# The filter network of a long-convolution kernel, fed by feature instead of by position

## The chip, the cores and the metric

The kernel runs on one core of a Trainium2 chip. The metric is the device time of one execution, in microseconds (us). The times shown are medians of several executions, and the profile is of one execution taken by the hardware profiler. The engines are named as the profile names them: PE is TensorE's matmul side and PEld its weight loads, DVE is VectorE, ACT is ScalarE, POOL is GpSimd, SP is SyncE, which here only issues transfers. A name with a "q" behind it (SPq, ACTq) is the issuing of a transfer from that engine's queue.

## What is computed

A long convolution and, on its result, a feed-forward block. Cut to what matters, with 2 sequences of 12480 positions and 128 channels:

```python
h_filt = (np.maximum(pos_emb @ w1, 0.0) @ w2) * np.exp(-0.01 * pos)[:, None]   # the filter, 12480 x 128
u = x * v
y = causal_convolution(u, h_filt)          # along positions, a channel at a time, by FFT
x2 = (x * y).reshape(24960, 128)
h = x2 @ w_in                              # 128 -> 2048
g = (a0 + a1*h + a2*h**2 + a3*h**3) / (1 + |b0|*|h| + |b1|*h**2 + 1e-6)
out = g @ w_out                            # 2048 -> 128
```

pos_emb is 12480 x 64, w1 is 64 x 64, w2 is 64 x 128. The two weights w_in and w_out come as 64-bit floats and are turned into 32-bit ones on the chip. The exponential decay falls below the smallest 32-bit float, so only the first 82 runs of 128 positions have a filter other than zero.

## The kernel before, in words

The work is in three stretches.

**The filter stretch** is the loop at L534 to L557 of the program. Position 128*m + n2 is held as row m (82 rows, `MF`) and residue n2 (128 of them, in two sides: 64 to 127, and 63 down to 0). A block `i` is four residues of each side (`NP` = 4), so there are 16 blocks. A block goes through these steps:

- `load_pos` (L274 to L282) loads the 82 rows of the positional embedding for four residues of each side, position on the partitions. It is four transfers from SP (a load of 80 rows and one of 2, for each side).
- `hf_w` (L480 to L489) multiplies by the decay on DVE, in two instructions, one a side. The decay (`win`) was loaded once, at L285.
- `hf_t` (L491 to L506) turns the block with four PE transposes, so that the 2 x 64 features lie on the partitions and 4 x 82 = 328 positions along the row. ACT copies it out of PSUM (L506).
- `hf_1` (L508 to L512) multiplies by w1 (twice on the diagonal of `bdw1`), and ACT takes the relu out of PSUM (L512). The decay is positive, so it can stand before the relu.
- `hf_2` (L514 to L524) multiplies by w2 with sum and difference of the two sides (`bdw2`), and four ACT instructions put the result into `hf`.

In iteration i the program issues `hf_t(i)`, `hf_1(i-1)` and `hf_2(i-2)`; it has 18 iterations. Every engine executes its own instructions in the order in which they are written, so what else is written in this loop stands in the same queues:

- `scalars` (L369 to L445), a generator, works out the constants of the rational function from moe_a and moe_b by a chain of tiny DVE instructions on 128x1 columns of the tile `sc`, with ACT for absolute values and a square root. Two of its steps stand in each iteration.
- `weights_gen` (L447 to L472), another generator, converts the weights in 16 pieces of 128x256. Step k: `to_f32` (L326 to L345) of piece k is seven DVE instructions (four one-input integer ones in 0.28 us each at L333, L335, L336, L339, another at L341, and two-input ones at L338 and L342) and a POOL addition (L344); `normal` (L349) of piece k-1 on DVE; for the first eight pieces two ACT instructions (L462, L463) that scale and round piece k-1 to `win_h`; and a POOL subtraction (L458) that leaves the remainder of piece k-2 in `win_l`. One step stands in each iteration from i = 5 on, so 13 of the 18 steps (k = 0 to 12) lie in this stretch. The tile `fa` has two buffers: L342 of piece k writes where L458 of piece k-2 read.
- `load_u` and `mult_u` load pieces of x and v and multiply them, on POOL (L248) for i < 8.
- PSUM is one pool of four tiles of two banks, used in turn.

**The convolution of sequence 0** (L602 to L643) runs over 32 groups of four channels, with a pipeline of four stages. Its DVE instructions are L173, L174, L205, L206, L566, L567 and L571 to L574, and in its first 24 iterations also a piece of x times v (L248, on DVE there). Steps of `weights_gen` that are left are taken in the iterations after that (L640).

**The second part** (L649 on) does the convolution of sequence 1 and the feed-forward block of both sequences by a fixed plan of work items.

A weight-step's end and the filter's end meet in the DVE queue: the convolution's first DVE instruction (L566) is queued behind the last weight step of the filter stretch, and needs the whole of `hf` through PE (L155).

Of the kernel before, what the change touches and what calls it, by code (L numbers as in the profile page):

```python
# [9 lines left out]
F32 = mybir.dt.float32  # L10
# [11 lines left out]
M = 98  # L22
# [40 lines left out]

def constants():
# [31 lines left out]
    win = win.reshape(M, N2)[:96]  # L96
# [14 lines left out]
def build(ctx: ExitStack, tc, x, x_q, v_q, pos_emb, w1, w2, w_in, w_out, moe_a, moe_b,  # L111
# [148 lines left out]
    with ExitStack() as st:  # L260
# [4 lines left out]
        win, bdw1, bdw2 = flat[0][0:96, 0:N2], flat[1][:, 0:128], flat[2][:, 0:2 * D]  # L265
# [5 lines left out]
        NPL = 4  # L271
        pos_t = {}

        def load_pos(p0):  # L274
            t = sp.tile([M, 2 * NPL, FO], F32, tag="wa", name="pos", bufs=3)
            for o, t0 in ((0, H2 + p0), (NPL, H2 - p0 - NPL)):
                if MF < M:
                    for r0, r1 in ((0, MF // 16 * 16), (MF // 16 * 16, MF)):
                        nc.sync.dma_start(out=t[r0:r1, o:o + NPL], in_=rows(pos_emb, r0, r1 - r0, t0, NPL, 0, FO))
                else:  # L280
                    load_rows(t[:, o:o + NPL], pos_emb, t0, NPL, 0, FO, True)
            pos_t[p0] = t  # L282
# [43 lines left out]
        def to_f32(raw, n):  # L326
# [4 lines left out]
            fa = sp.tile([128, n], F32, tag="f", name="f", bufs=2)  # L331
# [29 lines left out]

        def ts(o, i, s1, op0, s2=None, op1=None):
            kw = {} if op1 is None else {"op1": op1}
            nc.vector.tensor_scalar(out=col(o), in0=col(i), scalar1=s1, scalar2=s2, op0=op0, **kw)

        def tt(o, i, j, op):
            nc.vector.tensor_tensor(out=col(o), in0=col(i), in1=col(j), op=op)

        def scalars():  # L369


            for i in range(4):
                col(f"a{i}")
            for i in range(2):
                col(f"b{i}")
            nc.scalar.dma_start(out=sc[:, 0:4], in_=moe_a.unsqueeze(0).to_broadcast([128, 4]))
            nc.scalar.dma_start(out=sc[:, 4:6], in_=moe_b.unsqueeze(0).to_broadcast([128, 2]))
            for n in ("a0", "a1", "a2", "a3", "b0", "b1"):
                nc.scalar.activation(out=col("m" + n), in_=col(n), func=AF.Abs)
            tt("sum", "ma0", "ma1", ALU.add)  # L380
            tt("sum", "sum", "ma2", ALU.add)
            tt("sum", "sum", "ma3", ALU.add)
            yield

            ts("d", "ma3", 1e-30, ALU.max)
            nc.vector.reciprocal(out=col("d"), in_=col("d"))
            tt("q", "ma2", "d", ALU.mult)
            tt("q", "q", "ma2", ALU.mult)
            ts("lim", "sum", 16.0, ALU.mult)
            tt("flag", "q", "lim", ALU.is_le)  # L390
            ts("q", "ma3", 1024.0, ALU.mult)
            tt("q", "q", "sum", ALU.is_ge)
            yield
            tt("flag", "flag", "q", ALU.mult)
            ts("q", "mb1", 1e-9, ALU.is_ge)
            tt("flag", "flag", "q", ALU.mult)
            ts("q", "mb1", 1e9, ALU.is_le)
            tt("flag", "flag", "q", ALU.mult)
            tt("q", "mb0", "mb0", ALU.mult)
            ts("lim", "mb1", 16.0, ALU.mult)  # L400
            tt("q", "q", "lim", ALU.is_le)
            tt("flag", "flag", "q", ALU.mult)
            yield
            ts("not", "flag", -1.0, ALU.mult, 1.0, ALU.add)

            tt("b1e", "mb1", "flag", ALU.mult)
            tt("b1e", "b1e", "not", ALU.add)
            tt("a3e", "a3", "flag", ALU.mult)
            tt("a3e", "a3e", "not", ALU.add)
            yield  # L410

            for o, i in (("eta", "b1e"), ("sb1", "mb1")):
                ts("d", i, 1e-30, ALU.max)
                nc.scalar.activation(out=col("d"), in_=col("d"), func=AF.Ln)
                nc.scalar.activation(out=col(o), in_=col("d"), func=AF.Exp, scale=0.5)
                for _ in range(2):
                    nc.vector.reciprocal(out=col("d"), in_=col(o))
                    tt("d", "d", i, ALU.mult)
                    tt("d", "d", o, ALU.add)
                    ts(o, "d", 0.5, ALU.mult)  # L420
                yield
# [25 lines left out]
        def weights_gen():  # L447
# [663 lines left out]
```

## Time and profile before

| what | value |
|---|---|
| three runs | 2212.48, 2213.13 (median), 2214.62 us |
| the profiled execution: time | 2212.58 us |
| its span from first to last instruction | 2210.8 us |
| busy: PE, DVE, ACT, POOL | 89%, 93%, 87%, 91% of the span |
| filter stretch (up to the first L566) | 78.5 us |

The last 1.8 us of the time lie outside of the span. The shares are means over three stretches that differ. A row of the timeline reads: start in us, duration in us, engine, line, operation, tile written <- tiles read, shape, and in brackets how long the engine had been idle before it and what ended that. A row of the windows reads: the stretch, its length, then for PE, PEld, DVE, ACT and POOL the busy us and the number of instructions, the granted TensorE clock (1.00 is 2.4 GHz, 0.50 is 1.2 GHz), the mean busy share of the 16 DMA engines, and GB/s.

### The profile page before, as it was taken

The numbers are of one execution on the slowest core, as the hardware profiler recorded it, in microseconds if no ns is written. First come the engines' busy times: TensorE is split into PE (matmuls) and PEld (weight loads), VectorE is DVE, ScalarE is ACT, GpSimd is POOL, SyncE is SP. The second block draws the span as 40 slices with busy tenths as digits, with TensorE's granted clock in tenths as the row PEclk, the third lists the DMA queues.
The fourth block names the chain that finished last, engine by engine and source line by source line (L and its number), as shares of the span: only waits on it lengthen the run. The fifth ranks groups of instructions, "written<-read, shape, count | busy, mean of one in ns | idle before, by whom it ended". The sixth has DMA issues, their size and how long they took to land.

```text
span 2210.8 us, 25117 instructions
## 1 busy us (share of the span) xinstructions
PE 1966.8 (89%) x8352; PEld 1316.6 (60%) x8352; DVE 2067.0 (93%) x2354; ACT 1918.0 (87%) x1939; POOL 2015.8 (91%) x1605
## 2 busy tenths in 40 slices
PE   6899987899999999999999888888888888888886
PEld 4678766566666666666666555545545544555543
DVE  6899994899999998999999899999999999999997
ACT  5422223999999999999999899999999999999997
POOL 5477755999999999999999789999999999999998
PEclk9999988999999999999999999999999999999999
DMA  5344325443143233222222121221112111221100
GB/s 162 109 134 156 114 82 143 113 99 77 37 114 86 52 81 87 75 67 75 56 62 53 49 48 32 48 48 33 41 37 39 48 31 33 48 49 33 36 10 10
DMA packets 148283, 149.61 MB, mean 68 GB/s; under 512 B 88766, under 2 KB 117824, under 8 KB 145264
## 3 DMA queue, kind: packets, MB, share of 16 engines
q1 hardware_dynamic: 141120, 124.16, 22.4%
q10 hardware_dynamic: 7024, 23.76, 3.3%
q8 instruction: 68, 1.11, 0.2%
q14 instruction: 71, 0.58, 0.1%
HBM read 99.72 MB, written 48.17 MB: 67 GB/s over the span
## 4 chain that ended last, share of the span: by engine, by line
POOL 39%; ACT 20%; DVE 16%; PE 9%; issue 4%; DMA 0%; POOLq 0%; DVEq 0%; ACTq 0%
POOL v L986 20%; POOL v L980 9%; ACT v L915 5%; ACT r L964 4%; ACT l L959 4%; POOL q L954 4%; DVE q L970 4%; PE acc L995 3%; DVE q L975 3%; DVE v L925 3%; ACT q L891 3%; ACT q L943 3%; POOL q L953 2%; PE cv L823 2%; PE h L881 1%
## 5 line engine op out<-in xcount | busy, mean ns | idle before, releaser
L986 POOL TENSOR_TENSOR v<-v,q 128x970 f32<-128x970 f32 (+3 forms) x416 | 935.1, 2253 | 13.6 <-DVE q L975 12.7
L995 PE MATMUL acc<-v,wout 128*128 128x485 f32 (+3 forms) x1664 | 766.7, 584 | 126.3 <-POOL v L986 118.4
L925 DVE SCALAR_TENSOR_TENSOR v<-v,sc,h 128x970 f32<-128x970 f32 (+3 forms) x416 | 502.5, 1208 | 24.3 <-ACT q L891 22.5
L970 DVE SCALAR_TENSOR_TENSOR q<-q,sc,r 128x970 f32<-128x970 f32 (+3 forms) x416 | 502.1, 1207 | 22.7 <-ACT r L964 20.1
L995 PEld LDWEIGHTS acc<-v,wout 128*128 128x128 f32 x1664 | 293.6, 192 | 372.8 <-POOL v L986 183.6
L975 DVE SCALAR_TENSOR_TENSOR q<-q,r 128x970 f32<-128x970 f32 (+3 forms) x416 | 479.2, 1152 | 11.1
L881 PE MATMUL h<-ahi,win_l 128*128 128x486 f32 (+3 forms) x832 | 410.5, 493 | 45.8 <-DVE v L925 42.9
L915 ACT ACTIVATE v<-h,sc 128x970 f32<-128x970 f32 (+3 forms) x416 | 437.6, 1085 | 14.0 <-PE h L883 13.8
L964 ACT ACTIVATE r<-l 128x970 f32<-128x970 f32 (+3 forms) x416 | 416.6, 1001 | 16.9 <-DVE q L975 15.9
L980 POOL TENSOR_SCALAR v<-v,sc 128x980 f32<-128x980 f32 (+6 forms) x321 | 421.1, 1312 | 0.1
L959 ACT ACTIVATE l<-q,sc 128x1940 f32<-128x1940 f32 (+3 forms) x208 | 400.7, 1927 | 2.4 <-POOL q L954 2.1
L882 PE MATMUL h<-alo,win_h 128*128 128x486 f32 (+3 forms) x832 | 320.2, 385 | 0.0
L883 PE MATMUL h<-ahi,win_h 128*128 128x486 f32 (+3 forms) x832 | 318.9, 383 | 0.0
L891 ACT ACTIVATE q<-h 128x970 f32<-128x970 f32 (+3 forms) x303 | 303.3, 1001 | 2.8 <-POOL v L986 2.3
L881 PEld LDWEIGHTS h<-ahi,win_l 128*128 128x128 f32 x832 | 158.0, 190 | 208.6 <-DVE v L925 135.2
L882 PEld LDWEIGHTS h<-alo,win_h 128*128 128x128 f32 x832 | 158.8, 191 | 49.5 <-issue 34.2
L943 ACT ACTIVATE q<-q,sc 128x1940 f32<-128x1940 f32 (+2 forms) x95 | 185.6, 1953 | 0.0
L883 PEld LDWEIGHTS h<-ahi,win_h 128*128 128x128 f32 x832 | 158.8, 191 | 26.0
L948 ACT ACTIVATE q<-q,sc 128x1470 f32<-128x1470 f32 (+3 forms) x113 | 170.3, 1507 | 0.0
L823 PEld LDWEIGHTS cv<-yc,gt 90*98 90x98 f32 x1004 | 119.9, 165 | 26.2 <-issue 10.9
L823 PE MATMUL cv<-yc,gt 90*98 90x128 f32 x1004 | 128.1, 274 | 3.8 <-DVE an L829 3.5
L954 POOL TENSOR_TENSOR q<-q 128x490 f32<-128x490 f32 (+3 forms) x113 | 111.0, 982 | 9.4
(113 smaller groups left out, 2623.6 us busy)
## 6 DMA issues: line engine op xcount, KB each, us to landing
yc<-y_d SPq DMA_DIRECT2D x23, 900.0 KB
gt<-in_g_dram SPq DMA_DIRECT2D x48, 344.5 KB
xq<-in_x_q_dram SPq DMA_DIRECT2D x64, 196.0 KB
vq<-in_v_q_dram SPq DMA_DIRECT2D x64, 196.0 KB
h_d<-hg ACTq DMA_DIRECT2D x32, 360.0 KB
y_d<-ys ACTq DMA_DIRECT2D x16, 720.0 KB
hg<-h_d SPq DMA_DIRECT2D x64, 180.0 KB
y_d<-ys SPq DMA_DIRECT2D x16, 720.0 KB
```

Source lines behind the costliest of these rows:

```text
L881: nc.tensor.matmul(out=t[:, k, 0:w], lhsT=wl, rhs=hi[:, 0:w], start=True, stop=False)
L882: nc.tensor.matmul(out=t[:, k, 0:w], lhsT=wh, rhs=lo[:, 0:w], start=False, stop=False)
L883: nc.tensor.matmul(out=t[:, k, 0:w], lhsT=wh, rhs=hi[:, 0:w], start=False, stop=True)
L915: nc.scalar.activation(out=v, in_=st_h[s, i], func=AF.Square, bias=col("s"))
L925: stt(out=v, in0=v, scalar=col("k"), in1=h, op0=ALU.add, op1=ALU.mult)
L959: nc.scalar.activation(out=part(st_l, s, i), in_=part(st_q, s, i), func=AF.Ln, **({"bias": col("ka")} if short else {}))
L964: nc.scalar.activation(out=t[:, :, 0:w], in_=halves(st_l[s], i, w), func=AF.Exp, scale=-1.0)
L970: nc.vector.scalar_tensor_tensor(out=q, in0=q, scalar=col("ka") if short else 0.0, in1=st_r[s, i], op0=ALU.add, op1=ALU.mult)
L975: nc.vector.scalar_tensor_tensor(out=q, in0=q, scalar=2.0, in1=st_r.pop((s, i)), op0=ALU.subtract, op1=ALU.mult)
L980: nc.gpsimd.tensor_scalar(out=v, in0=v, scalar1=col("p0" if short else "a0"), scalar2=1.0, op0=ALU.add, op1=ALU.mult)
L986: nc.gpsimd.tensor_tensor(out=v, in0=v, in1=halves(st_q[s], i, w), op=ALU.mult)
L995: nc.tensor.matmul(out=acc[j][:, 0:w], lhsT=wout[:, f, :], rhs=st_v[s][:, i, 0:w], start=(f == 0), stop=(f == NF - 1), skip_group_check=True)
```

## The change

The positional embedding and the decay are laid out by feature on the host: `pos_q` has for each of the 16 blocks a 128 x 328 array (side and feature on the partitions, positions along the row), and `win_d` has for each block and side one row of 328 decay values. A block is now loaded with three transfers: the 128 x 328 piece of `pos_q`, and for each side the decay row, repeated over 64 partitions. There are no transposes, no copy of them and no `hf_w`: PE multiplies the loaded piece by `bdw1`, and one DVE instruction takes relu and decay out of PSUM together. The loop has 17 iterations, with `hf_1(i)` and `hf_2(i-1)` in iteration i.

Beside that: the loads of moe_a and moe_b go first on the ACT queue; `scalars` is rewritten with two-operation instructions (39 on DVE in three steps, one step an iteration); `to_f32` has one DVE instruction less; `fa` has three buffers; the remainder `win_l` moves from POOL to DVE as one instruction that scales and subtracts; L462 goes; the weight steps start at i = 3, so that 14 of the 18 (k = 0 to 13) lie in this stretch; `ident` is loaded late.

```diff
         def load_pos(i):
+            if i < nb:
+                t = sp.tile([128, W], F32, tag="wa", name="pos", bufs=3)
+                w = sp.tile([128, W], F32, tag="wn", name="win", bufs=3)
+                nc.sync.dma_start(out=t, in_=pos_q[i])
+                for s in range(2):
+                    nc.sync.dma_start(out=w[s * FO:(s + 1) * FO], in_=win_d[i, s].unsqueeze(0).to_broadcast([FO, W]))
+                pos_t[i] = (t, w)
...
+        nc.scalar.dma_start(out=sc[:, 0:4], in_=moe_a.unsqueeze(0).to_broadcast([128, 4]))
+        nc.scalar.dma_start(out=sc[:, 4:6], in_=moe_b.unsqueeze(0).to_broadcast([128, 2]))
         load_pos(0)
-        nc.sync.dma_start(out=win, in_=win_d)
-        nc.sync.dma_start(out=ident, in_=ident_d)
-        load_pos(NPL)
...
+        load_pos(1)
+        load_pos(2)
...
-            V.tensor_scalar(out=ib, in0=hi, scalar1=signed(0xC0000000), scalar2=None, op0=ALU.bitwise_and)
...
-            V.tensor_tensor(out=ia, in0=ia, in1=ib, op=ALU.bitwise_or)
+            V.scalar_tensor_tensor(out=ia, in0=hi, scalar=signed(0xC0000000), in1=ia, op0=ALU.bitwise_and,
+                                   op1=ALU.bitwise_or)
...
-                        nc.gpsimd.tensor_tensor(out=win_l[:, o], in0=t, in1=win_h[:, o].bitcast(F32), op=ALU.subtract)
+                        nc.vector.scalar_tensor_tensor(out=win_l[:, o], in0=t, scalar=col("eta"),
+                                                       in1=win_h[:, o].bitcast(F32), op0=ALU.mult, op1=ALU.subtract)
...
-                        nc.scalar.activation(out=t, in_=t, func=AF.Identity, scale=col("eta"))
-                        nc.scalar.activation(out=win_h[:, (k - 1) * WN:k * WN], in_=t, func=AF.Identity)
+                        nc.scalar.activation(out=win_h[:, (k - 1) * WN:k * WN], in_=t, func=AF.Identity,
+                                             scale=col("eta"))
...
         def hf_1(i):
+            t, w = pos_t.pop(i)
             ps = cvs()
-            nc.tensor.matmul(out=ps[:, 1, 0:W], lhsT=bdw1, rhs=pT.pop(i), start=True, stop=True)
+            nc.tensor.matmul(out=ps[:, 1, 0:W], lhsT=bdw1, rhs=t, start=True, stop=True)
             rT[i] = ctile(sp, "zu", 2, CG).rearrange("p r c k -> p (r c k)")[:, 0:W]
-            nc.scalar.activation(out=rT[i], in_=ps[:, 1, 0:W], func=AF.Relu)
+            nc.vector.scalar_tensor_tensor(out=rT[i], in0=ps[:, 1, 0:W], scalar=0.0, in1=w, op0=ALU.max, op1=ALU.mult)
+            load_pos(i + 3)
...
+        nc.vector.tensor_scalar(out=bdw2[64:128, D:], in0=bdw2[64:128, D:], scalar1=-1.0, scalar2=None, op0=ALU.mult)
-        for i in range(nb + 2):
+        for i in range(nb + 1):
             if i < nb:
-                hf_t(i)
-            if 0 <= i - 1 < nb:
-                hf_1(i - 1)
-            if 0 <= i - 2 < nb:
-                hf_2(i - 2)
+                hf_1(i)
+            if i >= 1:
+                hf_2(i - 1)
...
-            for _ in range(2):
-                next(sg, None)
-            if i >= 5:
+            next(sg, None)
+            if i >= 3:
                 next(wg, None)
```

## Rows read from the trace of the kernel before

**Rows 1.** Windows: the filter stretch, a part of it, the convolution, one busy us.

```profile
0.00:76.00 76.00, 53.07 (x232) 34.86 (x233) 54.07 (x193) 50.84 (x126) 42.23 (x33) 0.93 0.50 150
20.00:30.00 10.00, 5.17 (x15) 3.41 (x16) 8.68 (x45) 3.75 (x10) 2.53 (x2) 0.66 0.54 170
150.00:200.00 50.00, 50.00 (x282) 40.76 (x281) 49.36 (x71) 13.39 (x24) 39.97 (x39) 1.00 0.49 152
11.00:12.00 1.00, 0.17 (x1) 0.17 (x2) 0.89 (x5) 0.48 (x3) 0.00 (x0) 1.00 1.06 340
```

**Rows 2.** Timeline of one iteration late in the filter stretch, DVE and POOL.

```profile
53.02 0.42 DVE L342 SCALAR_TENSOR_TENSOR f<-i,i 128x256 f32<-128x256 int32 x1 [0.63 <-POOL win_l L458]
...
53.53 0.83 POOL L344 TENSOR_TENSOR f<-f,i 128x256 f32<-128x256 f32 x1 [0.54 <-DVE f L342]
53.70 0.94 DVE L489 TENSOR_TENSOR pw<-pos,ta 82x256 f32<-82x256 f32 x1
...
54.33 2.59 POOL L458 TENSOR_TENSOR win_l<-f,win_h 128x256 fp32r<-128x256 f32 x1
...
54.57 0.41 DVE L349 SCALAR_TENSOR_TENSOR f<-i,f 128x256 f32<-128x256 int32 x1
...
56.95 0.42 DVE L342 SCALAR_TENSOR_TENSOR f<-i,i 128x256 f32<-128x256 int32 x1 [0.63 <-POOL win_l L458]
```

**Rows 3.** Timeline of the start of the filter stretch; last row: the group of small DVE instructions.

```profile
2.64 1.49 ACTq L292 DMA_DIRECT2D tb<-in_w_dram  x2
...
5.83 0.37 ACTq L376 DMA_DIRECT2D sc<-in_moe_a_dram  x1
...
8.77 0.48 ACT L379 ACTIVATE sc<-sc 128x1 f32<-128x1 f32 x4 [2.50 <-DMA sc<-in_moe_a_dram]
...
29.06 0.28 DVE L333 TENSOR_SCALAR i<-raw 128x256 int32<-128x256 int32 x1
...
L364 DVE TENSOR_SCALAR sc<-sc 128x1 f32<-128x1 f32 x18 | 2.7, 151 | 0.6
```

**Rows 4.** Timeline of the end of the filter stretch.

```profile
74.70 2.71 PE L155 MATMUL cs<-f,hf 82*128 82x180 f32 x16 [0.70 <-ACT hf L524]
75.02 0.42 DVE L342 SCALAR_TENSOR_TENSOR f<-i,i 128x256 f32<-128x256 int32 x1
...
76.28 0.42 DVE L349 SCALAR_TENSOR_TENSOR f<-i,f 128x256 f32<-128x256 int32 x1 [0.83 <-POOL f L344]
...
78.50 0.90 DVE L566 TENSOR_TENSOR tb<-cs,twh 128x720 f32<-128x720 f32 x1
```

**Rows 5.** Timeline of DVE late in the convolution: a left-over weight step, and an iteration without.

```profile
270.11 0.48 DVE L349 SCALAR_TENSOR_TENSOR f<-i,f 128x256 f32<-128x256 int32 x1
...
275.96 0.90 DVE L566 TENSOR_TENSOR tb<-cs,twh 128x720 f32<-128x720 f32 x1
...
319.08 0.91 DVE L566 TENSOR_TENSOR tb<-cs,twh 128x720 f32<-128x720 f32 x1 [0.52 <-POOL zu L180]
```

**Rows 6.** Timeline of POOL: the product of x and v, alone and beside DVE.

```profile
17.05 1.27 POOL L248 TENSOR_TENSOR hu<-xq,vq 98x512 f32<-98x512 f32 x1 [0.59 <-DMA vq<-in_v_q_dram]
...
36.14 3.14 POOL L248 TENSOR_TENSOR hu<-xq,vq 98x512 f32<-98x512 f32 x1
```

**Rows 7.** Timeline of DVE: products of a PSUM and an SBUF operand, two widths.

```profile
364.14 0.56 DVE L829 TENSOR_TENSOR an<-cv,xt 98x384 f32<-98x384 f32 x1 [4.44 <-PE cv L823]
...
366.82 0.42 DVE L829 TENSOR_TENSOR an<-cv,xt 98x256 f32<-98x256 f32 x1 [2.12 <-PE cv L823]
```

**Rows 8.** Timeline: matmuls of `hf_2` early and late, and one block's loads from SP.

```profile
26.58 3.52 PE L518 MATMUL cs<-tb,zu 128*82 128x256 f32 x8
...
55.69 1.89 PE L518 MATMUL cs<-tb,zu 128*82 128x256 f32 x8
...
56.60 1.47 SPq L279 DMA_DIRECT2D pos<-in_pos_emb_dram  x4
```

**Rows 9.** The groups of instructions: the ACT copy behind the transposes, all 16.

```profile
L506 ACT ACTIVATE zh<-cs 128x328 f32<-128x328 f32 x16 | 6.9, 434 | 6.0 <-PE cs L503 6.0
```

More of the change, by code (lines that the diff above doesn't have):

```diff
@@ L110, in build @@
 @with_exitstack
-def build(ctx: ExitStack, tc, x, x_q, v_q, pos_emb, w1, w2, w_in, w_out, moe_a, moe_b,
+def build(ctx: ExitStack, tc, x, x_q, v_q, pos_q, w1, w2, w_in, w_out, moe_a, moe_b,
           f1_d, tw_d, twh_d, dft_d, dfth_d, idfth_d, g_d, win_d, ident_d, out):
@@ L369, in scalars @@
         def scalars():
[L372 to L380, printed above, removed]
@@ L394, in scalars @@
[L394 to L406, printed above, removed]
@@ L407, in scalars @@
[L407 to L415, printed above, removed]
-                for _ in range(2):
[L417 to L421, printed above, removed]
@@ new lines, in scalars @@
+            mul, add, le, ge = ALU.mult, ALU.add, ALU.is_le, ALU.is_ge
+            nc.scalar.activation(out=cols("ma0", "mb1"), in_=cols("a0", "b1"), func=AF.Abs)
+            ts("sum", "ma0", "ma1", add, "ma2", add)
+            ts("lim", "sum", "ma3", add, 16.0, mul)
+            ts("sum", "sum", "ma3", add)
+            ts("d", "ma3", 1e-30, ALU.max)
+            V.reciprocal(out=col("d"), in_=col("d"))
+            ts("q", "ma3", 1024.0, mul, "sum", ge)
+            ts("d", "d", "ma2", mul, "ma2", mul)
@@ new lines, in scalars @@
+            ts("flag", "d", "lim", le, "q", mul)
+            ts("lim", "mb1", 16.0, mul)
+            ts("q", "mb0", "mb0", mul, "lim", le)
+            ts("flag", "mb1", 1e-9, ge, "flag", mul)
+            ts("flag", "mb1", 1e9, le, "flag", mul)
+            ts("flag", "flag", "q", mul)
+            ts("not", "flag", -1.0, mul, 1.0, add)
+            ts("b1e", "mb1", "flag", mul, "not", add)
+            ts("a3e", "a3", "flag", mul, "not", add)
+            i, o, d = cols("mb1", "b1e"), cols("sb1", "eta"), sc[:, 30:32]
@@ new lines, in scalars @@
+            V.tensor_scalar(out=d, in0=i, scalar1=1e-30, scalar2=None, op0=ALU.max)
+            nc.scalar.activation(out=d, in_=d, func=AF.Ln)
+            nc.scalar.activation(out=o, in_=d, func=AF.Exp, scale=0.5)
+            yield
+            for _ in range(2):
+                V.reciprocal(out=d, in_=o)
+                V.tensor_tensor(out=d, in0=d, in1=i, op=mul)
+                V.tensor_tensor(out=d, in0=d, in1=o, op=add)
+                V.tensor_scalar(out=o, in0=d, scalar1=0.5, scalar2=None, op0=mul)
@@ L447, in weights_gen @@
+            ts("dl", "mb0", "ie", mul, 0.5, mul)
+            ts("ka", "dl", "dl", mul, -1.0, mul)
+            ts("ka", "ka", C1, add)
+            V.tensor_copy(flag_i, col("flag"))
         def weights_gen():
@@ L524, in hf_2 @@
                 nc.scalar.activation(out=o, in_=a, func=AF.Identity)
-        hf_w(0)
-        load_pos(2 * NPL)
         sg = scalars()
@@ L548, in build @@
                 nc.sync.dma_start(out=idfth, in_=idfth_d)
-            if i == 0:
-                nc.vector.tensor_scalar(out=bdw2[64:128, D:], in0=bdw2[64:128, D:], scalar1=-1.0, scalar2=None, op0=ALU.mult)
-            for _ in range(2):
-                next(sg, None)
-            if i >= 5:
+                nc.sync.dma_start(out=ident, in_=ident_d)
+            next(sg, None)
+            if i >= 3:
                 next(wg, None)
@@ L1096 @@
     feeds = [("x", inputs["x"]), ("x_q", by_quarter(inputs["x"])), ("v_q", by_quarter(inputs["v"]))]
-    feeds += [(n, inputs[n]) for n in _INS[2:]] + list(constants().items())
+    feeds += [("pos_q", by_feature(inputs["pos_emb"]))] + [(n, inputs[n]) for n in _INS[3:]] + list(constants().items())
     for name, a in feeds:
```

116 lines of the change are left out of this document (35 added, 81 removed).

## The prediction

> **What bounds the kernel now.** I read the windows first, to see which engine is full in which stretch, then the timeline of the filter stretch, iteration by iteration, and last the queue around the first L566, where this stretch ends. In the convolution DVE is busy 49.4 of 50 us, so whatever starts it earlier, or leaves it less DVE work, comes off the total. In the filter stretch no engine is full: of 76 us DVE works 54, PE 53, ACT 51, POOL 42 [rows 1]. It is bound by a loop between DVE and POOL: an iteration takes 56.95 - 53.02 = 3.93 us, POOL is in it with L344 (0.83) and L458 (2.59), and L342 of the next piece waits 0.63 us for L458, whose buffer it writes. L458 itself is stretched: it stands from 54.33 on while DVE runs the chain behind L349. L489, with two SBUF inputs, takes 0.94 instead of the 0.41 of L349, another such instruction, and ends just behind L344 [rows 2]. The first weight step starts only at 29.06 us [rows 3], 13 of them lie in this stretch, and behind the last one L566 follows at 78.50, while its data (L155, from 74.70) are there some 1 us earlier [rows 4]. So the stretch ends with DVE's queue of weight steps, and the filter is nearly as late.
>
> The sum is made against the profiled execution, 2212.58 us, which is 0.55 us under the median of the three runs.
>
> **Part 1, the start.** Removed are 26 of the 65 small DVE instructions, the wait for the loads of moe_a and moe_b (ACT stood 2.50 us for them, to 8.77), and eight `hf_w` instructions ahead of 29.06. Now DVE begins with the sign of `bdw2`, so it waits for w2, and everything on DVE is queued behind that. Its issue ended at 2.64 + 1.49 = 4.13 [rows 3]; two issues move ahead of it, at 1.47/4 = 0.37 each [rows 8], so 4.87. No row shows this landing alone. The nearest is moe_a, from its issue's end at 6.20 to its use at 8.77, 2.57 us [rows 3]; below, nothing lands before it is issued. I take 2.6, so 7.4, and 0.6 more for sign and first relu: 8.0. The 39 small instructions cost 0.151 each [rows 3] and a gap, 0.19 taken: 3.2, 3.0 and 1.1 us for the three steps. Between the first two DVE waits for two ACT instructions: two hand-overs at 0.51 (L342 to L344 [rows 2]), 1.0. POOL's product of x and v holds back two-input instructions for up to 1.27 [rows 6]; I take 1.0. With two more relus at 0.42 the first weight step starts at 8.0 + 3.2 + 1.0 + 3.0 + 1.0 + 1.1 + 0.8 = 18.1, say 18.2, instead of 29.06.
>
> **Part 2, a weight step.** From L342 to the next L349 it is 76.28 - 75.02 = 1.26 us when nothing but L344 lies between. From L349 to the end of L342's slot it is 78.50 - 76.28 = 2.22, of which L342 itself is 0.34 and the instruction that goes (L335, integer, one input) 0.2; the rest is 1.68 [rows 4]. Into the 1.26 fits the new relu. No row has it: the nearest are products of PSUM and SBUF, 0.42 at 256 columns and 0.56 at 384 [rows 7], so 0.50 for 328, some 0.42 of the queue; between these bounds it makes no difference, since it lies behind L344. The moved `win_l` has two SBUF inputs like L489 and will stand until L344 ends: 0.51 + 0.83, and 0.21 from L344's end at 54.36 to L349 at 54.57 [rows 2], so 1.55. The period is then 1.55 + 1.68 = 3.2 with `win_l`, and 1.26 + 1.68 = 2.95 without. L458's 2.59 and the 0.63 of waiting go altogether; late next is L344.
>
> While POOL still has L248 (iterations 3 to 7) it comes between two L344. Alone it takes 1.27, beside DVE's chain 3.14 [rows 6]: it gives way until DVE pauses. It then runs behind L342, and L344 behind it: 0.34 + 1.27 + 0.83 + 0.2 + 1.68 = 4.3. Bounds: 3.2, if it is wholly hidden, and 0.51 + 0.83 + 3.14 + 0.2 + 1.68 = 6.4, if all of 3.14 stood in the loop; I take 4.3, since DVE's own chain is what stretched it.
>
> By the Trainium skill (SBUF — State Buffer, Who interferes with whom) the one that starts first keeps the shared port pair for one whole instruction, and the other waits for that. The row disagrees: 1.87 us are more than any one of the DVE instructions there. By the page L248 would get in after one of them and hold DVE for 1.27, giving 4.5 a step and 2196 us.
>
> **Part 3, the end of the stretch.** Five steps at 4.3 from 18.2: 39.7; five at 3.2: 55.7; three at 2.95: 64.5. L333 to L566 is 1.7, so L566 starts at 66.2. The filter must be there too: the last relu follows the L342 two steps earlier, at about 60.4; 0.5 for it, 1.89 for `hf_2` [rows 8], four ACT copies, 2 us, and the first matmuls of L155, 1.35, half of 2.71 [rows 4]: 66.2 if all are waited for, 64.7 for the first copy alone. Both paths end together. Gain: 78.5 - 66.2 = 12.3.
>
> **Part 4, the convolution.** Piece 13 no longer lies there. A left-over step takes 275.96 - 270.11 = 5.85 us of the full DVE; without it 0.52 of waiting for POOL reappears [rows 5]: 5.3. Two steps with L335 remain, 0.2 each: 0.4.
>
> **What costs nothing.** 64 PE transposes, their copies (0.434 each [rows 9]), the relu on ACT and L462 go from engines that wait in this loop. PE's work per block is then 1.89 and the w1 matmul, a third of its columns: 2.5 us, under every period. SP issues three transfers a block instead of four, at 0.37; with one of weights and two of x and v, 2.2 us, under 2.95, so nothing queued behind waits long. The decay, loaded 16 times, adds 16 x 128 x 328 x 4 bytes = 2.7 MB to 150 GB/s x 76 us = 11.4 MB: 14.1 MB in 66 us are 214 GB/s, against 340 in a busy us [rows 1]. A block is asked for three periods ahead, at least 9 us; in front of it there is at most 1 MB (2.9 us at 340), and 2.6 for landing and 2.2 for issues make 7.7.
>
> Sum: 12.3 + 5.3 + 0.4 = 18.0. 2212.58 - 18.0 = 2194.6; with the 0.55, **2195 us**.
>
> **Rivals.**
> (a) POOL's L248 hides, and so does `win_l`: five steps at 3.2 and eight at 2.95 save 6.8 more; 2188, or 2186 with w2 landing sooner. For it: DVE has relu and waits in which POOL can work. Against: L489 stands behind L344 in every iteration seen.
> (b) A new wait in the place of the old: SP issues in order and stands behind loads of x and v that wait for POOL, so blocks arrive late and all steps take 4.3. That adds 5 x 1.1 + 3 x 1.35 = 9.6; 2205. For it: 7.7 of 9 us is little room. Against: x and v end at iteration 7.
> (c) PE stays at 1.2 GHz. Between 20 and 30 us, where it waited for DVE, the granted clock was 0.66 [rows 1], and `hf_2` took 3.52 instead of 1.89 [rows 8]. A block then takes 3.52 + 1.13 (656 of 2048 columns) = 4.65, 13 of them 60.5 instead of 46.3: 2209 if throughout, 2202 for half. Against: with 1.5 us of waiting per iteration, late in the stretch, `hf_2` had its 1.89.
> (d) Slower: the decay's rows, each read 64 times over by one transfer, come slowly. No row has such a large repeated load. Without them the 13 blocks need 13 x 0.43 + 5 x 0.40 = 7.6 MB, 22.4 us at 340 GB/s. No gain is left when the 13 periods take 84.2 - 1.7 - 18.2 = 64.3, that is when 13 x 0.168 = 2.18 MB of decay take 41.9 us: below 52 GB/s it decides, and at 40 it is 2226. Against: the stretch, with all its small rows, has 150 GB/s at a share of 0.50 [rows 1], 300 at a full one.
>
> **How the numbers follow.** My forecast (2190 to 2200) has 0.60, (a) 0.12, (b) 0.12, (c) 0.09, (d) 0.05; 0.02 is left for what I don't see. About 0.2% (4.4 us) is what a measurement of this kernel can tell from no change. Faster: the forecast, (a), (b) and half of (c), 0.88; same 0.07; slower 0.05. The range reaches from (a) with an early w2, 2185, to (b), 2205; outside are (d), half of (c), half of (b) and a little of (a), together under 0.2.
>
> **What would show it.** Right: the first L333-like instruction near 18 us, weight steps 4.3, then 3.2, then 2.95 us apart, the subtraction to `win_l` on DVE some 0.8 to 0.9 long, DVE waiting for L344 and not for POOL's subtraction, the first convolution instruction near 66 us, and two left-over weight steps instead of three. Wrong: DVE's relu waiting for a transfer (b, d), or for PE at a granted clock under 0.7 (c). A shorter stretch with an unchanged total would mean that the convolution is not started by it.

## The result, and the profile after

The changed kernel takes **2194.37 us** (median of 6 runs, 2192.38 to 2197.73), the kernel before 2214.06 (6 runs, 2212.48 to 2214.62): a ratio of 0.9913, with a 95% interval of 0.9903 to 0.9922. It is faster, by 19.7 us; 18.0 were predicted, and 2195. The profiled execution took 2193.18 us, with a span of 2191.4, 19.4 under the span before.

The windows of the changed kernel, with the columns of [rows 1]: the filter stretch, three parts of it, the convolution.

```profile
0.00:62.00 62.00, 41.04 (x152) 24.52 (x152) 47.61 (x143) 34.33 (x71) 19.19 (x24) 1.00 0.83 224
20.00:30.00 10.00, 7.29 (x30) 4.24 (x28) 9.47 (x23) 7.73 (x17) 4.73 (x5) 1.00 0.89 240
20.00:50.00 30.00, 20.11 (x82) 12.19 (x80) 27.67 (x66) 19.18 (x40) 12.57 (x13) 1.00 0.96 242
40.00:50.00 10.00, 6.68 (x29) 4.15 (x27) 8.27 (x24) 5.57 (x12) 2.05 (x3) 1.00 1.00 245
150.00:200.00 50.00, 50.00 (x279) 40.50 (x278) 49.33 (x71) 11.90 (x21) 40.38 (x40) 1.00 0.46 142
```

The convolution is as full of DVE as before (49.33 of 50 us). In the filter stretch POOL has become small, PE keeps a granted clock of 1.00 between 20 and 30 us where it had 0.66 before [rows 1], and one thing is new: the DMA share. Between 40 and 50 us the DMA engines are busy all the time and move 245 GB/s. Before, 340 GB/s had been seen in one busy us [rows 1].

The timeline of the changed kernel, ACT's queue, DVE, POOL and PE: the start, the first weight step, one iteration while POOL still has its products of x and v, the waits for a transfer, the end of the stretch, and a left-over weight step in the convolution with POOL's instructions beside it.

```profile
1.69 4.07 ACTq L296 DMA_DIRECT2D ta<-in_w_dram  x2
...
5.79 1.31 ACTq L298 DMA_DIRECT2D tb<-in_w_dram  x2
...
9.53 0.22 DVE L485 TENSOR_SCALAR tb<-tb 64x128 f32<-64x128 f32 x1 [9.53 <-DMA tb<-in_w_dram]
...
19.23 1.41 POOL L255 TENSOR_TENSOR hu<-xq,vq 98x512 f32<-98x512 f32 x1 [1.47 <-DMA vq<-in_v_q_dram]
19.23 0.28 DVE L341 TENSOR_SCALAR i<-raw 128x256 int32<-128x256 int32 x1
19.43 1.36 DVE L343 TENSOR_SCALAR i<-raw 128x256 int32<-128x256 int32 x1
...
22.83 1.48 DVE L357 SCALAR_TENSOR_TENSOR f<-i,f 128x256 f32<-128x256 int32 x1 [0.43 <-POOL f L352]
24.23 0.28 DVE L341 TENSOR_SCALAR i<-raw 128x256 int32<-128x256 int32 x1
...
32.48 0.28 DVE L341 TENSOR_SCALAR i<-raw 128x256 int32<-128x256 int32 x1
...
34.08 0.49 DVE L465 SCALAR_TENSOR_TENSOR zu<-cs,win 128x328 f32<-128x328 f32 x1
34.30 0.73 POOL L352 TENSOR_TENSOR f<-f,i 128x256 f32<-128x256 f32 x1 [2.03 <-DMA vq<-in_v_q_dram]
34.48 0.83 DVE L439 SCALAR_TENSOR_TENSOR win_l<-f,sc,win_h 128x256 fp32r<-128x256 f32 x1
34.99 1.45 POOL L255 TENSOR_TENSOR hu<-xq,vq 98x512 f32<-98x512 f32 x1
35.24 1.49 DVE L357 SCALAR_TENSOR_TENSOR f<-i,f 128x256 f32<-128x256 int32 x1
36.65 0.28 DVE L341 TENSOR_SCALAR i<-raw 128x256 int32<-128x256 int32 x1
...
44.93 0.29 DVE L341 TENSOR_SCALAR i<-raw 128x256 int32<-128x256 int32 x1 [0.95 <-DMA raw<-in_moe_w_in_dram]
...
48.82 0.29 DVE L341 TENSOR_SCALAR i<-raw 128x256 int32<-128x256 int32 x1 [0.71 <-DMA raw<-in_moe_w_in_dram]
...
61.36 0.30 DVE L341 TENSOR_SCALAR i<-raw 128x256 int32<-128x256 int32 x1 [0.40 <-DMA raw<-in_moe_w_out_dram]
...
66.30 2.71 PE L162 MATMUL cs<-f,hf 82*128 82x180 f32 x16 [0.69 <-ACT hf L478]
...
68.92 0.90 DVE L514 TENSOR_TENSOR tb<-cs,twh 128x720 f32<-128x720 f32 x1
...
260.70 1.06 POOL L215 TENSOR_TENSOR yy<-pta,ptb 128x360 f32<-128x360 f32 x1
260.87 1.03 DVE L341 TENSOR_SCALAR i<-raw 128x256 int32<-128x256 int32 x1
261.71 1.00 POOL L216 TENSOR_TENSOR yy<-pta,ptb 128x360 f32<-128x360 f32 x1
261.82 1.04 DVE L343 TENSOR_SCALAR i<-raw 128x256 int32<-128x256 int32 x1
262.67 1.32 POOL L544 TENSOR_TENSOR ys<-qt 90x512 f32<-90x512 f32 x1
262.79 1.49 DVE L345 SCALAR_TENSOR_TENSOR i<-raw,i 128x256 int32<-128x256 int32 x1
263.95 1.45 POOL L545 TENSOR_TENSOR ys<-qt 90x512 f32<-90x512 f32 x1
264.20 1.35 DVE L347 TENSOR_SCALAR i<-raw 128x256 int32<-128x256 int32 x1
...
266.13 0.90 DVE L514 TENSOR_TENSOR tb<-cs,twh 128x720 f32<-128x720 f32 x1
```

L296 and L298 are the issues of w1 and w2, L485 is the sign of `bdw2`, L341 the first instruction of a weight step, L465 the new relu, L439 the moved `win_l`, L352 POOL's addition (L344 before), L357 was L349, and L514 was L566, the convolution's first instruction on DVE. The first weight step starts at 19.23 instead of 29.06 [rows 3], L514 at 68.92 instead of 78.50 [rows 4]. The first weight step takes 5.00 us, to 24.23: L343 and L357 stand behind POOL's L255. The iteration from 32.48 to 36.65 takes 4.17 us: `win_l` stands behind POOL's L352, and L357 behind POOL's L255. Three steps wait for `raw`, a transfer that the kernel before did not wait for there. And in the convolution the same four instructions that take 0.28 to 0.42 in nearly all steps of the stretch take 1.03 to 1.49 each; each of them starts behind an instruction of POOL and ends just behind that one's end.

For all runs of this study the traces give the same four milestones: the first L514; the time from there to the L514 of the last of the 32 pieces; from there to the third L934, a multiplication on POOL (`v<-v,q`) that the second part repeats 416 times; from there to the end of the span. In the kernel before, the same instructions are L566 and L986. The column of steps says how many weight steps are left over to the convolution.

| Kernel (one profiled execution each) | steps left | first L514 | convolution | to third L934 | rest | span |
|---|---|---|---|---|---|---|
| before | 3 | 78.50 | 256.23 | 63.57 | 1812.5 | 2210.8 |
| changed | 2 | 68.92 | 248.55 | 61.04 | 1812.9 | 2191.4 |
| e1 weights alone | 2 | 71.86 | 248.62 | 63.16 | 1813.2 | 2196.8 |
| e2 layout alone | 3 | 73.11 | 257.40 | 61.62 | 1812.2 | 2204.3 |
| e3 product on DVE | 2 | 68.19 | 248.54 | 62.35 | 1812.0 | 2191.1 |
| e4 decay once | 2 | 68.10 | 248.55 | 61.30 | 1814.7 | 2192.6 |
| e5 decay rows | 2 | 69.01 | 248.60 | 62.35 | 1813.1 | 2193.1 |
| e6 w first | 2 | 67.32 | 248.57 | 61.22 | 1816.7 | 2193.8 |
| e7 one step more left | 3 | 69.32 | 256.61 | 62.15 | 1811.8 | 2199.9 |
| e8 steps at the end | 0 | 66.46 | 238.57 | 65.37 | 1814.2 | 2184.6 |
| e10 combined | 0 | 64.50 | 238.54 | 65.08 | 1813.2 | 2181.3 |
| e11 after the loop | 0 | 66.94 | 238.55 | 62.89 | 1817.1 | 2185.5 |

So the 19.4 us of the span are 9.6 from the stretch, 7.7 from the convolution, 2.5 from the passage to the second part, and -0.4 from the rest. The rest scatters by 5 us from run to run, whatever comes before it; a single time of this kernel says nothing about an edit worth 2 us, and such edits are read from the first three columns.

### The profile page after: what moved, and what is told of

Its sections match the earlier page's. It is cut to its first block, busy times and chain, and to the rows that moved or that the text cites. A ratio compares the mean times of both kernels' runs of the same rounds, so it can differ in the third digit from the quotient of the medians.

```text
span 2191.4 us, 24862 instructions
## 1 busy us (share of the span) xinstructions
PE 1954.7 (89%) x8288; PEld 1303.7 (59%) x8288; DVE 2057.6 (94%) x2304; ACT 1904.9 (87%) x1892; POOL 1992.7 (91%) x1597
## 4 chain that ended last, share of the span: by engine, by line
POOL 30%; ACT 27%; DVE 19%; PE 16%; issue 5%; DMA 2%; SPq 0%; POOLq 0%; DVEq 0%; ACTq 0%
POOL v L934 15%; POOL v L928 7%; ACT v L863 7%; ACT r L912 6%; ACT l L907 6%; DVE q L918 4%; PE acc L943 3%; DVE q L923 3%; DVE v L873 3%; ACT q L839 3%; POOL q L902 3%; ACT q L896 2%; ACT q L891 2%; PE cs L162 2%; PE cv L771 2%
## 5 line engine op out<-in xcount | busy, mean ns | idle before, releaser
L934 POOL TENSOR_TENSOR v<-v,q 128x970 f32<-128x970 f32 (+3 forms) x416 | 935.2, 2254 | 13.7 <-DVE q L923 12.9
L771 PEld LDWEIGHTS cv<-yc,gt 90*98 90x98 f32 x1004 | 119.3, 164 | 27.4 <-DVE an L777 11.2
```

The source lines that it names most:

```text
L934: nc.gpsimd.tensor_tensor(out=v, in0=v, in1=halves(st_q[s], i, w), op=ALU.mult)
```

## Experiments

**Which half of the change does it?** e1 puts only the rewritten constants and weight steps into the kernel before (the 39 small instructions, `to_f32`, `win_l` on DVE, the early loads of moe_a and moe_b), e2 only the new layout into the old weight steps.

The bodies of `scalars`, `to_f32` and `weights_gen` are swapped whole; the loop then has, in e1 (on the kernel before):

```diff
-            for _ in range(2):
-                next(sg, None)
-            if i >= 5:
+            next(sg, None)
+            if i >= 4:
```

and in e2 (on the changed kernel):

```diff
-            next(sg, None)
-            if i >= 3:
+            for _ in range(2):
+                next(sg, None)
+            if i >= 4:
```

> The kernel before with the rewritten constants and weight steps alone (subtraction to win_l on DVE, three buffers of fa, steps from i = 4 on, so 14 of 18 in the filter stretch), the old layout with transposes kept. Theory (the loop between DVE and POOL bound the filter stretch, and a left-over weight step costs over 5 us of the convolution): steps of 3.93 become about 3.5 us, the first one starts near 20 us instead of 29, the first convolution instruction of DVE comes near 71 us instead of 78.5, and the convolution is 7 us shorter: about 2200 us. Rival (the new layout carries the gain, since transposes and copies go): 2210 us or more.

> The changed kernel with the constants and weight steps of the kernel before (13 steps in the filter stretch, the subtraction on POOL, two buffers of fa). Theory: the loop over POOL's subtraction still sets the steps at 3.9 to 4.1 us although PE, ACT and DVE have less to do; the first step starts near 26 us, the first convolution instruction of DVE near 75 us, the convolution is unchanged: about 2210 us. Rival (the layout carries the gain): steps of about 3.2 us, first convolution instruction near 66 us, about 2202 us.

e1: 2199.4 us (4 runs), ratio 0.9936 (0.9919 to 0.9952). e2: 2209.83 us (10 runs), ratio 0.9978 (0.9968 to 0.9988). In time, both came out as the theory had it. Together 0.64% and 0.22%, 0.86% of the 0.87% measured: within the intervals the two halves add up, and the larger one is not the network's layout but the constants and weight steps. e1 takes 6.6 us from the stretch and, with a third step no longer left over, 7.6 from the convolution; e2 takes 5.4 from the stretch and leaves the convolution 1.2 longer. In the stretch they do not add up: 6.6 and 5.4 are 12.0, where the profiled execution of the whole change has 9.6, with 2.06 us of waits for `raw` that neither half has.

**What makes the early steps 4.1 us long?** e3 has DVE do the product of x and v.

```diff
-                mult_u(nc.gpsimd)
+                mult_u(nc.vector)
```

> The changed kernel with the products of x and v in the filter loop on DVE instead of POOL. The changed kernel has weight steps of 4.1 to 4.2 us in iterations 3 to 7. Theory (POOL's product between two additions makes them): about 3.8 us each (3.1 and 0.7 for the product on DVE), first convolution instruction 1.5 us sooner, 67.4 instead of 68.9. Rival (the transfers make them: 1.0 MB an iteration at the 245 GB/s that the profile shows there is 4.1 us): they stay at 4.1, with DVE waiting for transfers.

2193.24 us (one run), L514 at 68.19. The five early steps went the theory's way: they took 19.3 us together (20.56 to 39.85), 3.9 each, instead of 21.6 (19.23 to 40.81), with 0.4 us of waits for `raw` in them. Little of it reached L514, since DVE waited 2.4 us more for `raw` in the two steps behind them. e10 (below) has the same edit from iteration 3 on and no such wait in these steps. Its timeline on DVE, L256 the product:

```profile
27.93 0.28 DVE L341 TENSOR_SCALAR i<-raw 128x256 int32<-128x256 int32 x1
...
29.52 0.68 DVE L256 TENSOR_TENSOR hu<-xq,vq 98x512 f32<-98x512 f32 x1
30.13 0.49 DVE L465 SCALAR_TENSOR_TENSOR zu<-cs,win 128x328 f32<-128x328 f32 x1
30.54 0.54 DVE L439 SCALAR_TENSOR_TENSOR win_l<-f,sc,win_h 128x256 fp32r<-128x256 f32 x1
31.00 0.41 DVE L357 SCALAR_TENSOR_TENSOR f<-i,f 128x256 f32<-128x256 int32 x1
31.34 0.28 DVE L341 TENSOR_SCALAR i<-raw 128x256 int32<-128x256 int32 x1
```

The period is 3.41 instead of 4.17, although DVE does 0.68 more: L357 is back at 0.41 from 1.49. e10 also loads the decay as different rows, but e5 (below), which does so and leaves the product on POOL, has 3.9 to 4.2 in the same steps. The early steps are long because of POOL's L255.

**Is it the decay that fills the DMA engines, and why?** e4 loads the decay of block 0 and uses it for all blocks (this changes what is computed). e5 loads all of it, but as one transfer of 128 different rows a block, laid out so in DRAM.

Their edits are, in e4 (`w0` is one tile for all blocks):

```diff
-                for s in range(2):
-                    nc.sync.dma_start(out=w[s * FO:(s + 1) * FO], in_=win_d[i, s].unsqueeze(0).to_broadcast([FO, W]))
-                pos_t[i] = (t, w)
+                if i == 0:
+                    for s in range(2):
+                        nc.sync.dma_start(out=w0[s * FO:(s + 1) * FO], in_=win_d[i, s].unsqueeze(0).to_broadcast([FO, W]))
+                pos_t[i] = (t, w0)
```

and in e5:

```diff
+    win = np.repeat(win, FO, axis=1)
...
-                for s in range(2):
-                    nc.sync.dma_start(out=w[s * FO:(s + 1) * FO], in_=win_d[i, s].unsqueeze(0).to_broadcast([FO, W]))
+                nc.sync.dma_start(out=w, in_=win_d[i])
```

> The changed kernel with the decay loaded for block 0 alone and used for all 16 blocks, so the filter is multiplied by the wrong decay from block 1 on; 2.5 MB less to load. Theory (full DMA engines make DVE wait 0.95, 0.71 and 0.40 us for raw weights in the later steps, and let w2 land as late as 9.5 us): these waits vanish, w2 lands near 8.5, and the first convolution instruction of DVE comes near 66 us instead of 68.9; iterations 3 to 7 stay at 4.1 to 4.2 if POOL makes them, and fall to 3.4 if the transfers do. Rival (the waits are SP's order, not bytes): they stay, 68 us or more.

> The changed kernel, with the decay laid out in DRAM as 128 rows per block and loaded by one transfer of 128 different rows, instead of two transfers that each read one row 64 times. The bytes into SBUF are the same, the result too. Between 20 and 50 us the changed kernel's DMA engines are full at 242 to 245 GB/s, and with the decay loaded once only they move 310 GB/s per full share (133 at 0.41, 193 at 0.62, 202 at 0.64). Theory: it is the 2.7 MB of rows of 1312 bytes that fill the engines, whoever reads them; then the share stays at 0.9 to 1.0 between 30 and 50 us, DVE goes on waiting for raw by 0.4 to 1.0 us in two or three steps, and L514 starts at 68.9 within 0.7. Rival: reading one row 64 times over is the slow part; then the share falls to 0.8 or less at the same bytes, the waits for raw are gone, and the stretch from the first weight step to L514, 49.7 us in the changed kernel, shortens to about 46.5, as with the decay loaded once (46.2).

The window from 20 to 50 us, of e4:

```profile
20.00:50.00 30.00, 22.77 (x90) 13.37 (x90) 29.18 (x77) 18.84 (x40) 11.96 (x12) 1.00 0.56 176
```

and of e5:

```profile
20.00:50.00 30.00, 21.63 (x87) 13.03 (x88) 29.16 (x78) 19.01 (x41) 11.96 (x12) 1.00 0.75 231
```

At a full share these are 176/0.56 = 314 GB/s without the decay, 231/0.75 = 308 with different rows, and 242/0.96 = 252 in the changed kernel, where one row is read 64 times over. In 30 us the changed kernel's engines are busy for 28.8 us and move 7.26 MB, e4's 16.8 us and 5.28 MB: the decay's 1.98 MB cost 12.0 us, as if at 165 GB/s. With different rows (e5 against e4) 1.65 MB cost 5.7 us, 290 GB/s. Both are estimates from differences, and they hold also what the other loads lost: packets of 2048 bytes, which are not the decay's, took 126 ns on average in this window of the changed kernel, 97 in e4 and 100 in e5; packets of 1312 bytes, embedding and decay, 83, 75 and 71. The other runs agree in the same window: at a full share the changed kernel, e3, e6, e7 and e8, all with repeated rows and shares of 0.93 to 0.97, have 243 to 267 GB/s, and e5, e10 and e11, with different rows and shares of 0.75 to 0.89, 284 to 308 (e2, with repeated rows at a share of 0.75, has 283). So the repeated reading is the slow part, as the rival had it, and the bytes alone are not.

The waits for `raw` are gone in both, e4's early steps still take 3.9 to 4.2 us, and from the first weight step to L514 it takes 46.2 and 46.3 us instead of 49.7. That the repeated rows caused the waits is argued, not shown. With repeated rows the changed kernel, e3, e6 and e7 waited 2.06, 2.78, 1.14 and 5.48 us for `raw`, but e8, the same code up to there, 0.06, and it took 47.2 from the first step to L514; with different rows e10 and e11 waited 0.35 and 1.13. And e4 and e5 also take issues from SP: there it issued the third to sixth `raw` 6.2 to 6.8 us ahead of their use, in the changed kernel 4.6 to 4.9. No run separates the two. The times, 2194.43 and 2194.94 us (one run each), show nothing of it, and L514 hardly moved, to 68.10 and 69.01: in both the start came later (w2 landed at 10.48 and 11.20 instead of 9.53, the first step at 21.86 and 22.75). w2's issue ended only 0.2 to 0.4 us later there; it landed 3.2 and 3.7 us behind that instead of 2.4. Why is open; SP issues the next loads earlier in these two.

**Does w2 land late because of its place in ACT's queue?** e6 issues moe_a and moe_b behind w1 and w2.

```diff
-        nc.scalar.dma_start(out=sc[:, 0:4], in_=moe_a.unsqueeze(0).to_broadcast([128, 4]))
-        nc.scalar.dma_start(out=sc[:, 4:6], in_=moe_b.unsqueeze(0).to_broadcast([128, 2]))
         load_pos(0)
...
+        nc.scalar.dma_start(out=sc[:, 0:4], in_=moe_a.unsqueeze(0).to_broadcast([128, 4]))
+        nc.scalar.dma_start(out=sc[:, 4:6], in_=moe_b.unsqueeze(0).to_broadcast([128, 2]))
         load_pos(1)
```

> The changed kernel, with the loads of moe_a and moe_b issued behind those of w1 and w2 on ACT's queue (as before the change) instead of ahead of them. Theory: w2 lands late (9.5 us instead of the 7.4 of the sum) because its issue is late and the DMA engines are full; with two issues of 0.37 less ahead of it the first DVE instruction (the sign of bdw2) starts 0.7 to 2.5 us sooner, between 7.0 and 8.8, and the first weight step at 17 to 18.5 instead of 19.2. Rival: w2's landing is set by the transfers that are under way, not by its place on ACT's queue; then the sign stays at 9.3 to 10, and the first step at 19.2 or later, because moe_a comes later too.

The timeline of e6, L296 the issues of w2:

```profile
2.21 2.47 ACTq L296 DMA_DIRECT2D tb<-in_w_dram  x2
...
7.02 0.22 DVE L485 TENSOR_SCALAR tb<-tb 64x128 f32<-64x128 f32 x1 [7.02 <-DMA tb<-in_w_dram]
...
9.36 0.21 ACT L385 ACTIVATE sc<-sc 128x6 f32<-128x6 f32 x1 [7.34 <-DMA sc<-in_moe_b_dram]
...
9.60 0.83 DVE L380 TENSOR_SCALAR sc<-sc 128x1 f32<-128x1 f32 x4 [1.82 <-ACT sc L385]
```

The place in the queue decides when w2 is there: 7.02, and 6.8 to 8.4 in the three other runs with this order (e2, e10, e11), against 9.3 to 11.2 in the six with the new layout and the changed kernel's order. It works through the issue: that ended at 4.68 instead of 7.10, and w2 landed 2.3 us behind it instead of 2.4. In the changed kernel ACT's queue stood for 3.0 us between the two issues of w1; for what, the profile doesn't show. But the small instructions then wait for moe_b, and the first step starts at 18.64, outside of what the theory said (17 to 18.5): of 2.5 us 0.6 are left. One wait replaced the other. The time, 2195.72 us in one run, lies in the scatter of the rest.

**What does a left-over step cost?** e7 begins the weight steps one iteration later, so that three are left over as before.

```diff
-            if i >= 3:
+            if i >= 4:
                 next(wg, None)
```

> The changed kernel with its weight steps begun one iteration later: 13 of them start in the filter stretch instead of 14, and three are left over to the convolution, as in the kernel before, with everything else of the change in place. Theory: a third left-over step costs the convolution more than its DVE work, since PE, waiting behind it, loses its clock: from L514 to the L514 of piece 31 it takes 248.6 us in the changed kernel and 257.4 in the kernel with three left over (the layout alone). The stretch gains 1.5 to 2.9 us, the convolution loses 7.7 to 8.9, so the time rises by 4.8 to 7.4, to 2199 to 2202 us. Rival, the sum as predicted: a left-over step costs its 5.3 us of DVE alone; then the time rises by 2.4 to 3.8, to 2196.5 to 2198.

2203.66 us (4 runs), ratio 0.9957 (0.9940 to 0.9974): 9.3 us more than the changed kernel, above both expectations. The convolution lost 8.1, as the theory said; the stretch, which should have gained 1.5 to 2.9, gained nothing, since DVE waited 5.5 us for `raw`. The timeline of e7 behind the third left-over step, PE and DVE:

```profile
296.37 3.69 PE L533 MATMUL cs<-idfth,yy 128*90 128x128 f32 x16 [6.61 <-DVE zh L522]
...
302.46 0.91 DVE L514 TENSOR_TENSOR tb<-cs,twh 128x720 f32<-128x720 f32 x1 [2.45 <-POOL yy L216]
```

and the same place in the kernel before:

```profile
306.30 3.64 PE L585 MATMUL cs<-idfth,yy 128*90 128x128 f32 x16 [6.88 <-DVE zh L574]
...
311.26 0.91 DVE L566 TENSOR_TENSOR tb<-cs,twh 128x720 f32<-128x720 f32 x1 [1.32 <-POOL yy L208]
```

PE waits 6.6 us for DVE, its next matmuls take 3.69 us instead of the 1.91 that they take at 2.4 GHz (the granted clock from 290 to 300 us is 0.59), and now DVE waits for what hangs on them. With two left-over steps the same happens to PE behind the first one:

```profile
270.20 3.43 PE L533 MATMUL cs<-idfth,yy 128*90 128x128 f32 x16 [4.91 <-DVE zh L522]
```

But there DVE has the second step to do meanwhile and doesn't wait, and behind the second one PE's longest wait is 1.5 us and its matmuls take 1.95. So the first two cost 10.0 us together (e8, below), and the third 8.1 more.

**Where would they cost nothing?** Pieces 14 and 15 are parts of `wout`, used from 376 us on. e8 moves them to the convolution's last three iterations, where DVE is idle for 12 of 20 us (325.3 to 345.6 in the changed kernel).

```diff
             if uw and gq * (uw[0][0] - 1) <= g:
                 mult_u(nc.vector)
-            else:
+            elif g >= NG:
                 next(wg, None)
```

> The changed kernel with its two left-over weight steps (pieces 14 and 15, used only from 376 us on) moved from the middle of the convolution, where DVE is full, to its last three iterations, where DVE is idle for 6 of 10 us and more. Theory: the left-over steps cost there 9.3 us of DVE and of PE's wait (seven pieces take 64.2 us instead of 7 x 7.85 = 55.0), and at the end they find idle time; L514 of piece 31 starts some 9 us sooner, at 308.5, and the time falls by 6 to 9 us, to 2185 to 2188. Rival: DVE's queue is in order, so the steps stand in front of the last pieces' products, and the chain of the last pieces is latency, not work; then 4 to 6 of the 9 us are given back between 310 and 350, and the time falls by 3 to 5 us. It can't be slower unless the second part's first instruction waits for the last step: then POOL's first L934, now at 368.3, stays there.

2188.03 us (4 runs), ratio 0.9886 (0.9869 to 0.9902): 6.3 under the changed kernel, at the near edge of the theory's range. But the way is the rival's: the convolution gave 10.0, and 4.3 came back in the passage. (In the profiled executions 2.5 us more come from the stretch, which this edit doesn't touch: there the waits for `raw` were gone.) The timeline of e8 on DVE, the first of the two steps and what it holds up:

```profile
320.24 1.03 DVE L341 TENSOR_SCALAR i<-raw 128x256 int32<-128x256 int32 x1
321.19 1.35 DVE L343 TENSOR_SCALAR i<-raw 128x256 int32<-128x256 int32 x1
...
323.66 0.90 DVE L212 TENSOR_TENSOR pta<-cs,hg 128x720 f32<-128x720 f32 x1
...
326.80 1.14 DVE L545 TENSOR_TENSOR ys<-qt 90x512 f32<-90x512 f32 x1 [1.43 <-DMA y_d<-ys]
...
336.74 0.56 DVE L777 TENSOR_TENSOR an<-cv,xt 98x384 f32<-98x384 f32 x1 [3.04 <-PE cv L771]
```

The last L514 is at 305.03, L777, the second part's first, at 336.74: 31.7 us, against 28.2 in the changed kernel (317.47 to 345.67). The step stands in front of L212, and behind that hangs the chain through POOL, PE and ACT to the first rows that the second part needs.

**A version that beats both?** e10 joins the edits of e5, e6 and e8 and, from iteration 3 on, that of e3:

```diff
-                mult_u(nc.gpsimd)
+                mult_u(nc.gpsimd if i < 3 else nc.vector)
```

e11 is e10 without the edit of e8; both left-over steps stand behind the convolution's loop instead, where the generator is run to its end:

```diff
             if uw and gq * (uw[0][0] - 1) <= g:
                 mult_u(nc.vector)
-            else:
-                next(wg, None)
             load_u()
         for _ in wg:
             pass
```

> The changed kernel with four edits at once: the two left-over weight steps in the convolution's last three iterations, w1 and w2 loaded ahead of moe_a and moe_b, the decay loaded as 128 different rows, and from iteration 3 on the product of x and v on DVE instead of POOL. Theory: each part keeps what it showed by itself. The start is that with w first (sign at 7.0, first weight step at 18.6); from there to L514 it took 46.3 with different rows of decay and no wait for raw, and the product on DVE takes some 1.4 off (47.6 less 2.8 of waits for raw); so L514 starts at 63.5 instead of 68.9 (66.5 in the run with the steps at the end), and the time is 6.3 + 3 to 5.4 below the changed kernel's 2194.4: 2182.5 to 2185. Rival: what limits the stretch is the DMA engines as a whole, and w2 lands late again (11.2, as with the different rows alone, where SP issues its loads sooner): then the first step is at 21 to 23, L514 at 66 to 68, and the time is 2186 to 2188.5, no better than with the steps at the end alone.

> As the combined kernel, but both left-over weight steps stand behind the convolution's last instruction on DVE instead of between its last pieces. Theory: with the steps between the last pieces the chain of these pieces (L213, POOL, PE, ACT, L545) became 3.5 us longer, from 37.6 to 41.1 us between the last L514 and the first L777... behind the loop the chain is as short as in the changed kernel, but the steps (6.5 to 7 us of DVE) then stand in front of L777, which could start some 4 us behind the loop's end; so L777 starts 2.5 to 3 us later than its data allow and the two arrangements come out within 1.5 us of each other. Rival: L777's delay is fully hidden by loads of x and g that are late anyway; then this one is 3 us faster than the combined kernel.

e10: **2184.76 us** (4 runs), ratio 0.9875 (0.9858 to 0.9891), 28.6 us under the kernel before (2213.32 beside it) and 9.6 under the changed one, whose interval lies above. Against e8 (up to 0.9902) it is not told apart by the times. L514 came at 64.50, 1.0 later than the theory had: w2 landed at 7.32, but DVE then stood 3.76 us for moe_b, and the first step was at 21.27, where the rival had it, though not for its reason. From there to L514 it took 43.2 us. e11: 2185.71 us (4 runs), ratio 0.9874 (0.9857 to 0.9890). Its passage is 2.2 us shorter than e10's, its L514 2.4 later, with 1.1 us of waits for `raw`; the two are within 1.5 us, as expected, and which place is better is not settled by the times. (The 37.6 and 41.1 us in the expectation were misread; they are the 28.2 and 31.7 above, with the same difference.)

## Why the prediction was right, and where its steps were not

The mechanism was right: the stretch ended with DVE's queue of weight steps, and a left-over step less came off the convolution. That the total was right within a microsecond is partly luck, since the terms missed both ways: 12.3 from the stretch and 5.7 from the convolution became 9.6, 7.7 and 2.5 from the passage behind it, which the sum did not have. The passage lies between 61.0 and 63.2 us in all the changed runs with steps left, so its 2.5 us are partly scatter; what sets them was not tried.

**Part 1, the start: the w2 term was mis-sized.** 7.4 was taken for its landing; it landed at 9.53. The 2.6 us from issue to landing were right, 2.4. What failed is the end of its issue, 4.87 in the sum, with 0.37 for each of the two issues that moved ahead: it was 7.10, since ACT's queue stood for 3.0 us ahead of w1's second issue, and e6 shows that this goes with the place behind moe_a and moe_b. (Of `hf_w`, 14 instructions stood ahead of 29.06 and not eight; no term hangs on that.) Half of it came back: from the sign to the first step it took 9.7 us where the sum had 10.8. So the first step was at 19.2, not at 18.2.

**Part 2, the step: right, in part by luck.** The relu is 0.49 (predicted 0.50), `win_l` 0.76 to 0.83 (0.8 to 0.9). The first period is 5.00, with two instructions held behind POOL's product, and the four behind it are 4.1 to 4.2 (predicted 4.3 for all five); together the five took 21.6 us where the sum had 21.5. The later periods without waits are 3.1 (3.2) and 2.9 (2.95). e10 and e5 show that POOL's product makes the early ones. The way is not quite the one described: POOL adds first, and the product then holds L357 for its whole 1.45 us, instead of running ahead of the addition. By the Trainium skill (SBUF — State Buffer, Who interferes with whom) that is the rule, one whole instruction; the row at 35.24 agrees with it, while the product of 3.14 us that the prediction set against it [rows 6] was held up for longer than one instruction, in the kernel before. The 4.5 us a step that the prediction drew from the rule were 0.3 to 0.4 too many for these four steps all the same, since L357 had its own 0.41 to do.

**Part 3, the end: right in kind, and hit by the loads.** 66.2 was predicted for L514, 68.92 came. e8 is the changed kernel up to 250 us, instruction for instruction, and there L514 came at 66.46, with 0.06 us of waits for `raw`. In the changed kernel's trace three such waits cost 2.06 us. The stretch ends with DVE's queue; the filter's data (L162, from 66.30) are there 1.3 us earlier, if half of its 2.71 is taken for the first piece.

**What costs nothing: the step that failed.** The decay was costed at nothing, with 214 GB/s against 340 in a busy us. That us held none of the decay's repeated rows; with them a full engine share moves 243 to 267 GB/s here, and the decay costs engine time as if at 165. This is rival (b), blocks that come late, in small: 0.1 to 2.1 us in two executions of the same code, not 9.6, and it struck `raw`, not the blocks. Its cause may be (d)'s slow rows, far above the 52 GB/s from which (d) would have decided, or, as in (b), SP's issues in order; e4 and e5 change both.

**Part 4, the convolution: a term too small.** 5.7 was predicted, 7.7 measured. The step's own time was about right (5.0 each for two of them), but behind the third DVE also waits, 2.45 us in e7, for PE at its lower clock, which the iterations looked at in [rows 5] don't hold. Why a step costs 5.0 there and 2.94 in the stretch is in its own rows: L341 to L347 take 1.03 to 1.49 each, one behind each of POOL's L215, L216, L544 and L545 (1.00 to 1.45), while POOL is busy for 8 of 10 us. The same section of the Trainium skill says that even instructions with one SBUF input can take the shared port pair in their faster modes; L341, with one input, agrees.

**The rivals.** (a) would need L255 hidden; it stood in each of the five steps. (c) did not occur: the granted clock was 1.00 in the windows up to 62 us, and only the first block's `hf_2`, at 10.33, took 3.66 us instead of 1.9.

## What to carry to other kernels

Ask of each piece of work not only how long it takes but beside what: a weight step cost 2.94 us in one stretch, 5.0 in another and 8.1 as the last of three there, and moving two of them to where their engine idles was worth as much as a third of the whole change. Ask of a transfer that reads one row many times what it does to the others, and cost it by the full share of the engines, not by one busy microsecond. Where a single time scatters by more than an edit is worth, read the edit's milestones in the trace instead.

## What was not expected of the hardware

- Rows of 1312 bytes read 64 times over each cost the DMA engines time as if at 165 GB/s, different rows of that length as if at 290 (estimates from differences of runs); the packets of other loads took 126 ns beside the repeated rows and 100 beside the different ones.
- The same code waited 2.06 us for its weights in one execution and 0.06 in another, and 5.5 us when the steps were one iteration later.
- PE's loss of clock can cost twice: after 6.6 us of waiting its next 16 matmuls took 3.69 us instead of 1.91 (granted clock 0.59), and DVE, the engine that bounds the convolution, then waited 2.45 us for what follows from them.
